# Whole 128-row tiles, GpSimd drains and adding transfers in a pooled-attention and mixture-of-experts kernel

## The chip, the cores and the metric

The kernel runs on one core of a Trainium2 chip. The metric is the device time of one execution in microseconds (us). Engines are TensorE (matrix products), VectorE, ScalarE, GpSimd (POOL in the rows) and SyncE (SP), which here only issues transfers. Data moves by 16 DMA engines, fed by a hardware queue (transfers issued on SyncE) and a software queue (transfers issued on GpSimd).

## The reference

Attention with pooled keys and values over 8 batches of 8 heads, 576 tokens and a head width of 64, then a mixture of 8 experts with top-1 routing, then a three-way gated layer, all in float32:

```python
k_p = k.reshape(B, H, Sp, pool, D).mean(axis=3)      # pool = 8, Sp = 72
v_p = v.reshape(B, H, Sp, pool, D).mean(axis=3)
scores = scale * np.matmul(q, k_p.transpose(0, 1, 3, 2))
attn = np.exp(scores - np.max(scores, axis=-1, keepdims=True))
attn = attn / (np.sum(attn, axis=-1, keepdims=True) + 1e-09)
x = np.matmul(attn, v_p)                             # then [4608, 512]
# experts: xn @ en.T / tau, argmax, gate = softmax at the argmax
out[mask] = gate_w[mask, None] * (np.maximum(x[mask] @ w1[e], 0.0) @ w2[e])
# second layer
h = np.maximum(np.maximum(x @ w1, x @ w2), x @ w3);  result = h @ w_out
```

## The kernel before

Three stages follow each other. **Attention** takes 36 tiles of 128 query rows. The 576 pooled key rows of a batch (8 heads by 72) lie in five chunks of 128, 128, 128, 128 and 64 rows (`RC`). One turn of `for it in range(NT + 4)` issues stages of several tiles: scores (`stage_s`, names `psc`), exponentials (`stage_e`), transposes of the weights into `paT` and the copy into `aT` (`stage_a`), transposes of the queries (`stage_q`, `pqT`), and the product of `aT` with the values (`stage_x`, `pav`, L496). VectorE takes the row maxima, subtracts them and scales the result (L457 to L523), and beside that works on the routing of earlier tiles. A float32 pass of TensorE appears twice in the rows, a transpose once.

The values stand in `vbds`, spread out over head slots with a column of ones and 8 columns for the routing logits (73 columns a head). Chunk 4 has 64 rows and one head, so two of a tile's twelve recorded `pav` passes, and parts of `trans_kv` (L318), `trans_v` (L341) and `vdot` (L350), use 64 of the array's 128 rows.

**Pooling** is a sum over 8 rows. `load_rows` brings a batch's keys (`kraw`) and values (`vraw`) on SyncE, 1,024 KB and 128 KB each. For the first batches VectorE reduces part of it; from there GpSimd adds halves of each row three times (`pool_k2`, `pool_v`: w = 4, 2, 1, that is 256, 128 and 64 columns), chunk by chunk. Then `spread_v` (L293) writes the values to `vbds`. `kraw` and `vraw` have two buffers each, so a load waits for the adds of the batch two before it. The dictionary `todo` holds for each `it` the jobs of a batch; a batch b is first needed on TensorE at `need = (b // 2) * 9 + (0 or 4)`. On GpSimd everything runs in the order in which it was issued.

**The experts** (L1062, L1110) follow, and then **the second layer** (`second`) in 6 groups of 768 tokens: nine chunks of products, then six output tiles j = 0 to 5 of a group (`out_part`, L1697), each scaled by ScalarE (L1703) and written by an indirect scatter that GpSimd issues (`out_rows`, L1704). After the last group the kernel ends with drains and semaphores of all engines (rows with L1802).

Of the kernel before, what the change touches and what calls it, by code (L numbers as in the profile page):

```python
# [21 lines left out]
def attention_moe_moe_kernel(  # L22
# [32 lines left out]
    J = 8  # L55
# [60 lines left out]
    if True:  # L116
# [61 lines left out]
        if True:  # L178
# [7 lines left out]
            kv = {}  # L186

            def load_rows(pool_tag, src, b, sizes, apart=False, step=4):
                t = kvp.tile([P, 5, J, D], F32, tag=pool_tag, name=f"{pool_tag}{b}")
                flat = src[b].rearrange("h (s j) d -> (h s) (j d)", j=J)  # L190
                full = 0 if apart else sum(1 for n in sizes if n == P)
                for c in range(0, full, step):
                    e_ = min(c + step, full)
                    nc.sync.dma_start(
                        t[:, c:e_].rearrange("p c j d -> p c (j d)"),
                        flat[c * P : e_ * P].rearrange("(c p) x -> p c x", p=P),
                    )
# [37 lines left out]
            kbds = [ap1.tile([P, H, 2, SP], F32, name=f"kbd{i}") for i in range(3)]  # L235
            vbds = [ap1.tile([P, NSL, DA], F32, name=f"vbd{i}") for i in range(3)]
            nc.gpsimd.memset(kbds[0], 0.0)
            rmask = ap1.tile([P, 5, H], F32, name="rmask")
# [15 lines left out]
            def prep_steps(b):  # L254
                kt, vt = kv[b]
                kb, vb = kbds[b % 3], vbds[b % 3]
                kp = qp.tile([P, 5, 2, D], F32, tag="kp", name=f"kp{b}")
                vp = kp[:, :, 1, :] if b > 1 else qp.tile([P, 5, D], F32, tag="vp", name=f"vp{b}")
                vT = qp.tile([D, 5, P], F32, tag="vT", name=f"vT{b}", bufs=1)

# [12 lines left out]
                def pool_k2(sizes=RC, c0=0):  # L273
                    for c, n in list(enumerate(sizes))[c0:]:
                        for w in (4, 2, 1):
                            dst = kt[0:n, c, 0:w, :] if w > 1 else kp[0:n, c, 0:1, :]
                            nc.gpsimd.tensor_tensor(dst, kt[0:n, c, 0:w, :], kt[0:n, c, w : 2 * w, :], op=A.add)
# [5 lines left out]
                def pool_v(c0, c1, n):  # L283
                    for c in range(c0, c1):
                        for w in (4, 2, 1):
                            dst = vt[0:n, c, 0:w, :] if w > 1 else vp[0:n, c : c + 1, :]
                            nc.gpsimd.tensor_tensor(dst, vt[0:n, c, 0:w, :], vt[0:n, c, w : 2 * w, :], op=A.add)
# [24 lines left out]
                def trans_kv(cs, r0):  # L312
# [3 lines left out]
                    for c in cs:  # L316
                        n = RC[c]
                        nc.tensor.transpose(  # L318
                            ps[:, col : col + n], kp[0:n, c].rearrange("p two d -> p (two d)"), ident[0:n, 0:n]
                        )  # L320
                        col += n
                    a0 = 0
                    while a0 < col:
# [10 lines left out]
                        a0 = a1  # L334
                    nc.scalar.copy(vT.rearrange("p c r -> p (c r)")[:, r0 : r0 + col], ps[D:P, 0:col])

                def trans_v(c0, c1):
                    ps = pq.tile([P, 512], F32, tag="pq", name=f"ptv{b}_{c0}")
                    for c in range(c0, c1):
                        n = RC[c]  # L340
                        nc.tensor.transpose(  # L341
                            ps[0:D, (c - c0) * P : (c - c0) * P + n], vp[0:n, c, :], ident[0:n, 0:n]
                        )
                    w_ = (c1 - c0 - 1) * P + RC[c1 - 1]
                    nc.scalar.copy(vT.rearrange("p c r -> p (c r)")[:, c0 * P : c0 * P + w_], ps[0:D, 0:w_])

                def vdot():
                    ps = pq.tile([P, 512], F32, tag="pq", name=f"pd{b}")
                    for c, (h0, h1) in enumerate(HS):
                        nc.tensor.matmul(  # L350
                            ps[0 : RC[c], SL[c] * E : SL[c + 1] * E],
                            vT[:, c, 0 : RC[c]],
                            enT[:, h0:h1, :].rearrange("p h e -> p (h e)"),
                            start=True,
                            stop=True,
                        )
                    for n, s0, s1 in ((P, 0, SL[4]), (64, SL[4], NSL)):
                        nc.vector.tensor_tensor(
                            vb[0:n, s0:s1, D + 1 : DA],
                            ps[0:n, s0 * E : s1 * E].rearrange("p (s e) -> p s e", e=E),  # L360
                            mslot[0:n, s0:s1, :].to_broadcast([n, s1 - s0, E]),
                            op=A.mult,
                        )

# [103 lines left out]
            def stage_a(i):  # L468
# [3 lines left out]
                for c, n in enumerate(RC):  # L472
                    nc.tensor.transpose(ps[0:n, c * P : (c + 1) * P], at[:, c * P : c * P + n], ident)
                aT = ap2.tile([P, 5, P], F32, tag="aT", name=f"aT{i}")
                nc.scalar.copy(aT[:, 0:4, :], ps[:, 0 : 4 * P].rearrange("p (c n) -> p c n", n=P))
# [12 lines left out]
            def stage_x(i):  # L488
# [892 lines left out]
            p0[0]()  # L1381
            enT = ap1.tile([D, H, E], F32, name="enT")

            def en_steps():
# [4 lines left out]
                for h in range(H):  # L1389
                    nc.tensor.transpose(ps[0:D, h * E : (h + 1) * E], en[:, h * D : (h + 1) * D], ident[0:E, 0:E])  # L1390
                nc.scalar.copy(enT, ps[0:D, 0 : H * E].rearrange("p (h e) -> p h e", e=E))

# [75 lines left out]
            for b in range(1, B):  # L1468
                need = (b // 2) * 9 + (0 if b % 2 == 0 else 4)
                at_ = [need - 7, need - 3, need - 1, need, need, need + 1, need + 2]  # L1470
                at_ = {1: [2, 4, 6, 7], 2: [5, 6, 6, 7, 7, 7, 8, 9, 10]}.get(b, at_[:4] + at_[5:6])
                for j, t in enumerate(at_):
                    todo.setdefault(t, []).append((b, j))
# [7 lines left out]
            for it in range(NT + 4):  # L1481
# [90 lines left out]
    def second(st, groups, again=False):  # L1572
# [144 lines left out]
        for g in groups:  # L1717
# [89 lines left out]
```

## Time and profile before

| | us |
|---|---|
| median of 3 runs (1242.42 to 1244.53) | 1244.08 |
| profiled execution | 1242.23 |
| its span | 1240.2 |
| granted clock, mean (share of 2.4 GHz) | 0.995 |

| engine | busy us | share of the span |
|---|---|---|
| TensorE | 1205.1 | 97% |
| VectorE | 795.3 | 64% |
| ScalarE | 579.9 | 47% |
| GpSimd | 318.1 | 26% |

The span runs from the first instruction to the last; the profiled execution's own time is 2.0 us longer. Busy shares are means over stages. TensorE's weight loads (PEld) overlap its matrix passes, and the ends of passes are modelled, so that gaps are read better from the starts of weight loads. "[0.27 <-issue]" behind a row is idle time before it and what ended it; "issue" means that nothing in the profile released it. A shape like 64\*128 is the rows by columns of the array that are used.

### The profile page before, as it was taken

The page shows a single profiled execution, that of the slowest core. Times are in us where ns is not written, and L with a number is a line of the kernel's source. Part 1 is how long each engine was busy: PE and PEld are TensorE (multiplying, and loading weights), DVE is VectorE, ACT ScalarE, POOL GpSimd, SP SyncE. Part 2 cuts the span into 40 slices and gives each one's busy share as a digit, 9 for nine tenths or more (in the row PEclk, how much of TensorE's full clock was granted, in tenths as well). Part 3 has the DMA queues.
Part 4 walks back from the last instruction along what each step waited for, and adds up shares of the span by engine and source line. Part 5 has one row for each costly group of instructions (what it writes and reads, how often), then busy time and mean ns, then how long its engine had stood idle before and what let it go on. Part 6 is the DMA issues. An engine that isn't in the chain of part 4 may idle for free. (4 is left out here: it accounts for less than half of the span.)

```text
span 1240.2 us, 22423 instructions
## 1 busy us (share of the span) xinstructions
PE 1205.1 (97%) x8251; PEld 1149.6 (93%) x8251; DVE 795.3 (64%) x1597; ACT 579.9 (47%) x1040; POOL 318.1 (26%) x471
## 2 busy tenths in 40 slices
PE   6999999999999999999999999999999999999995
PEld 5888889899999999999998998998998998998994
DVE  5878886977789999987854445454454454453540
ACT  4666574445566666666654323324223223233221
POOL 6999534401122212121001202003004004004001
PEclk9999999999999999999999999999999999999998
DMA  9796344607884456555349665574673773773721
GB/s 261 222 341 205 137 145 155 198 23 138 296 279 154 138 213 221 205 204 158 124 146 307 253 241 209 193 254 173 231 264 146 256 262 122 259 286 107 262 97 53
DMA packets 98054, 246.21 MB, mean 199 GB/s; under 512 B 17116, under 2 KB 58122, under 8 KB 89874
## 3 DMA queue, kind: packets, MB, share of 16 engines
q1 hardware_dynamic: 84786, 189.09, 45.0%
q0 software_dynamic: 13152, 55.62, 13.4%
q8 instruction: 67, 1.10, 0.4%
q14 instruction: 49, 0.40, 0.1%
HBM read 252.23 MB, written 46.98 MB: 241 GB/s over the span
## 5 line engine op out<-in xcount | busy, mean ns | idle before, releaser
L1621 PE MATMUL p<-yhi,wt 128*128 128x384 f32 x1512 | 387.1, 336 | 0.0
L1621 PEld LDWEIGHTS p<-yhi,wt 128*128 128x128 f32 x1512 | 273.4, 188 | 0.7 <-PE pyT L1132 0.3
L1621 PE MATMUL p<-ylo,wt 128*128 128x384 f32 x756 | 254.0, 336 | 0.0
L1629 ACT COPY s<-p 128x384 f32<-128x384 f32 x162 | 77.8, 480 | 221.6 <-PE p L1621 214.2
L1110 PE MATMUL py<-hhi,wlo 128*128 128x256 f32 x576 | 163.1, 283 | 1.6 <-DVE wlo L1042 1.6
L1110 PE MATMUL py<-hhi,whi 128*128 128x256 f32 x576 | 164.6, 286 | 0.0
L1062 PE MATMUL ph<-xhi,whi 128*128 128x256 f32 x576 | 163.8, 284 | 0.7 <-DVE hlo L1078 0.7
L1062 PE MATMUL ph<-xhi,wlo 128*128 128x256 f32 x576 | 163.0, 283 | 0.7 <-DVE wlo L1042 0.7
L1062 PE MATMUL ph<-xlo,whi 128*128 128x256 f32 x576 | 163.0, 283 | 0.0
L1110 PE MATMUL py<-hlo,whi 128*128 128x256 f32 x576 | 162.9, 283 | 0.0
L1621 PEld LDWEIGHTS p<-ylo,wt 128*128 128x128 f32 x756 | 142.1, 188 | 0.5
L1650 DVE TENSOR_TENSOR blk<-p,s 128x384 f32<-128x384 f32 x108 | 59.7, 553 | 113.8 <-PE p L1621 113.5
L1606 POOL DMA_INDIRECT gt<-gbuf,ix x26 | 37.0, 1423 | 315.6 <-DMA ix<-idbuf 309.2
L1110 PEld LDWEIGHTS py<-hhi,wlo 128*128 128x128 f32 x576 | 110.4, 192 | 1.8 <-DVE wlo L1042 1.8
L1062 PEld LDWEIGHTS ph<-xhi,whi 128*128 128x128 f32 x576 | 110.5, 192 | 1.3 <-DVE hlo L1078 1.1
L1062 PEld LDWEIGHTS ph<-xhi,wlo 128*128 128x128 f32 x576 | 110.5, 192 | 0.9 <-DVE wlo L1042 0.9
L1062 PEld LDWEIGHTS ph<-xlo,whi 128*128 128x128 f32 x576 | 110.5, 192 | 0.0
L1110 PEld LDWEIGHTS py<-hlo,whi 128*128 128x128 f32 x576 | 110.5, 192 | 0.0
L1110 PEld LDWEIGHTS py<-hhi,whi 128*128 128x128 f32 x576 | 110.4, 192 | 0.0
L1042 DVE TENSOR_TENSOR wlo<-w2raw,whi 128x1024 fp32r<-128x1024 f32 x84 | 102.1, 1220 | 8.6 <-ACT whi L1040 8.5
L1042 DVE TENSOR_TENSOR wlo<-w1raw,whi 128x1024 fp32r<-128x1024 f32 x67 | 81.7, 1219 | 26.2 <-ACT whi L1040 25.3
L1040 ACT CAST whi<-w2raw 128x1024 fp32r<-128x1024 f32 x88 | 91.8, 1043 | 7.4 <-PE py L1110 4.4
(317 smaller groups left out, 2260.1 us busy)
## 6 DMA issues: line engine op xcount, KB each, us to landing
wt<-wdram SPq DMA_DIRECT2D x51, 1792.0 KB
w1raw<-in_moe_w_dram SPq DMA_DIRECT2D x88, 512.0 KB
w2raw<-in_moe_w_dram SPq DMA_DIRECT2D x88, 512.0 KB
wdram<-wst POOLq DMA_DIRECT2D x9, 1792.0 KB
ybuf<-yo SPq DMA_DIRECT2D x40, 256.0 KB
cvraw<-in_moe_w_dram POOLq DMA_DIRECT2D x36, 256.0 KB
xbuf<-x SPq DMA_DIRECT2D x16, 512.0 KB
yr<-ybuf SPq DMA_DIRECT2D x20, 384.0 KB
```

Of the source, the lines that this page charges most:

```text
L1040: nc.scalar.copy(hi, src)
L1042: eng.tensor_tensor(lo, src, hi.bitcast(F32), op=A.subtract)
L1062: nc.tensor.matmul(ps[:, f, :], a_[:, c, fs], b_[:, c, :], start=(n == 0), stop=(n == 3 * DC - 1))
L1110: nc.tensor.matmul(py[:, c // 2, (c % 2) * 256 : (c % 2 + 1) * 256], a_[:, f, c * P : (c + 1) * P], b_[:, f, :], start=(piece == 0 and f = ...
L1606: nc.gpsimd.indirect_dma_start(out=gt[g][:, j : j + 1], out_offset=None, in_=gbuf[:, :], in_offset=bass.IndirectOffsetOnAxis(ap=cols[j], a ...
L1621: nc.tensor.matmul(ps, a_, b_, start=(start and c + n == 0), stop=(c == 1 and n == 2), skip_group_check=True)
L1629: nc.scalar.copy(t, ps)
L1650: tt(src, add[0], add[1], op=A.add)
```

## The change

Three things change. First, what had 64 rows now has 128: `aT`, `kp`, `vp`, `vT`, `enT` and the last slots of `vbds` are fixed buffers whose unused rows are set to zero at the start, and the passes on them (`trans_kv`, `trans_v`, `vdot`, `pav`) run over all 128 rows. `vT` and `enT` keep their data in rows 64 to 127. The two VectorE products behind `vdot` become one.

Second, GpSimd gets a `drain` after the fourth output tile of each of the six groups.

Third, from the fourth batch on (b of 3 to 7) SyncE loads only the first 4 of the 8 rows to be summed, as pieces of 1 KB, and GpSimd issues four transfers a batch that add the other 4 rows to them in the buffer (`accum_op`), 20 in all. GpSimd then adds only twice (w = 2, 1). The transfers are issued in the turn `need - 9`.

```diff
+            HJ = J // 2
+            NFULL = 3
+            def row_parts(src, b, t, j0):
+                flat = src[b].rearrange("h (s j) d -> (h s) j d", j=J)
+                yield (
+                    t[:, 0:4, 0:HJ].rearrange("p c j d -> p c (j d)"),
+                    flat[0 : 4 * P, j0 : j0 + HJ].rearrange("(c p) j d -> p c (j d)", p=P),
+                )
+                yield t[0 : RC[4], 4, 0:HJ].rearrange("p j d -> p (j d)"), flat[4 * P :, j0 : j0 + HJ].rearrange("p j d -> p (j d)")
+            def load_half(pool_tag, src, b):
+                t = kvp.tile([P, 5, J, D], F32, tag=pool_tag, name=f"{pool_tag}{b}")
+                for dst, rows_ in row_parts(src, b, t, 0):
+                    nc.sync.dma_start(dst, rows_)
+                return t
+            def add_half(src, b, t):
+                for dst, rows_ in row_parts(src, b, t, HJ):
+                    nc.gpsimd.dma_start(dst, rows_, accum_op=A.add)
...
+            aTs = [ap1.tile([P, 5, P], F32, name=f"aT{i}") for i in range(2)]
+            kps = [qp.tile([P, 5, 2, D], F32, name=f"kp{i}", bufs=1) for i in range(2)]
...
+            for t_ in aTs:
+                nc.vector.memset(t_[R4:P, 4, :], 0.0)
+            for t_ in vbds:
+                nc.vector.memset(t_[R4:P, SL[4] : NSL, :], 0.0)
...
-                        for w in (4, 2, 1):
+                        for w in (4, 2, 1) if b < NFULL else (2, 1):
...
-                            ps[:, col : col + n], kp[0:n, c].rearrange("p two d -> p (two d)"), ident[0:n, 0:n]
+                            ps[:, col : col + P], kp[:, c].rearrange("p two d -> p (two d)"), ident
...
-                            ps[0 : RC[c], SL[c] * E : SL[c + 1] * E],
-                            vT[:, c, 0 : RC[c]],
+                            ps[:, SL[c] * E : SL[c + 1] * E],
+                            vT[:, c, :],
...
-                    for n, s0, s1 in ((P, 0, SL[4]), (64, SL[4], NSL)):
-                        nc.vector.tensor_tensor(
...
+                    nc.vector.tensor_tensor(
+                        vb[:, :, D + 1 : DA],
...
-                                aT[0 : RC[c], c, lo:hi],
-                                vbds[b % 3][0 : RC[c], sl : sl + g1 - g0, :].rearrange("p h d -> p (h d)"),
+                                aT[:, c, lo:hi],
+                                vbds[b % 3][:, sl : sl + g1 - g0, :].rearrange("p h d -> p (h d)"),
...
+                if b >= NFULL:
+                    todo.setdefault(need - 9, []).append(
+                        lambda b=b: (add_half(k, b, kv[b][0]), add_half(v, b, kv[b][1]))
+                    )
...
-                    kv[kvnext] = (load_rows("kraw", k, kvnext, RC), load_rows("vraw", v, kvnext, RC))
+                    if kvnext < NFULL:
+                        kv[kvnext] = (load_rows("kraw", k, kvnext, RC), load_rows("vraw", v, kvnext, RC))
+                    else:
+                        kv[kvnext] = (load_half("kraw", k, kvnext), load_half("vraw", v, kvnext))
...
                 out_rows(g, p_, j)
+                if j == 3:
+                    nc.gpsimd.drain()
```

The order of TensorE's 7,742 passes, and of SyncE's transfers, stays the same. On GpSimd two places matter. The first is behind the spread of batch 1 (`vbd_168`), where before the adds of batch 2's values (`vraw_257`) came at once:

```order
L293 TENSOR_TENSOR vbd_168<-vp_350,mslot 128x2x64
L293 TENSOR_TENSOR vbd_168<-vp_350,mslot 128x3x64 x3
L293 TENSOR_TENSOR vbd_168<-vp_350,mslot 64x64
L287 TENSOR_TENSOR vraw_257<-vraw_257 128x256
L287 TENSOR_TENSOR vraw_257<-vraw_257 128x128
L287 TENSOR_TENSOR kp_530<-vraw_257 128x64
```

In the changed kernel the adding transfers of batch 3 (`kraw_391`, `vraw_394`) stand between; batch 2's values are called `vraw_273` there:

```order
L330 TENSOR_TENSOR vbd_168<-vp_175,mslot 128x2x64
L330 TENSOR_TENSOR vbd_168<-vp_175,mslot 128x3x64 x3
L330 TENSOR_TENSOR vbd_168<-vp_175,mslot 64x64
L207 DMA kraw_391<-in_k_dram 128x4x256
L207 DMA kraw_391<-in_k_dram 64x256
L207 DMA vraw_394<-in_v_dram 128x4x256
L207 DMA vraw_394<-in_v_dram 64x256
L324 TENSOR_TENSOR vraw_273<-vraw_273 128x256
L324 TENSOR_TENSOR vraw_273<-vraw_273 128x128
L324 TENSOR_TENSOR kp_172<-vraw_273 128x64
```

So four issues, and their waits for SyncE's loads of batch 3, stand ahead of batch 2's adds. The second place is between batches 3 and 4 on GpSimd; before, the spreads of batch 2 (`vbd_169`) and batch 3 (`vbd_167`) were followed by batch 4's keys (`kraw_646`):

```order
L293 TENSOR_TENSOR vbd_169<-kp_530,mslot 128x2x64
L293 TENSOR_TENSOR vbd_169<-kp_530,mslot 128x3x64 x3
L293 TENSOR_TENSOR vbd_169<-kp_530,mslot 64x64
L293 TENSOR_TENSOR vbd_167<-kp_614,mslot 128x2x64
L293 TENSOR_TENSOR vbd_167<-kp_614,mslot 128x3x64 x3
L293 TENSOR_TENSOR vbd_167<-kp_614,mslot 64x64
L277 TENSOR_TENSOR kraw_646<-kraw_646 128x256
L277 TENSOR_TENSOR kraw_646<-kraw_646 128x128
L277 TENSOR_TENSOR kp_936<-kraw_646 128x64
```

Now the transfers of batch 4 (`kraw_644`, `vraw_647`) are issued between the two spreads, and batch 4's adds follow:

```order
L330 TENSOR_TENSOR vbd_169<-kp_172,mslot 128x2x64
L330 TENSOR_TENSOR vbd_169<-kp_172,mslot 128x3x64 x3
L330 TENSOR_TENSOR vbd_169<-kp_172,mslot 64x64
L207 DMA kraw_644<-in_k_dram 128x4x256
L207 DMA kraw_644<-in_k_dram 64x256
L207 DMA vraw_647<-in_v_dram 128x4x256
L207 DMA vraw_647<-in_v_dram 64x256
L330 TENSOR_TENSOR vbd_167<-kp_173,mslot 128x2x64
L330 TENSOR_TENSOR vbd_167<-kp_173,mslot 128x3x64 x3
L330 TENSOR_TENSOR vbd_167<-kp_173,mslot 64x64
L314 TENSOR_TENSOR kraw_644<-kraw_644 128x128
L314 TENSOR_TENSOR kp_172<-kraw_644 128x64
```

Only one spread lies between the issue of a batch's adding transfers and its first add, and the 256-column add is gone. Batches 5 to 7 repeat this.

## Rows read from the trace of the kernel before

**Rows 1.** The page, busy time of each engine over the span

```profile
PE 1205.1 (97%) x8251; PEld 1149.6 (93%) x8251; DVE 795.3 (64%) x1597; ACT 579.9 (47%) x1040; POOL 318.1 (26%) x471
```

**Rows 2.** Busy time by stretch: us, engines, granted clock, DMA share, GB/s

```profile
62.00:93.00 31.00, 30.80 (x249) 27.78 (x248) 23.49 (x65) 19.25 (x49) 28.64 (x62) 1.00 1.06 341
186.00:217.00 31.00, 31.00 (x251) 30.24 (x252) 18.66 (x36) 15.27 (x25) 13.43 (x9) 1.00 0.46 155
```

**Rows 3.** Timeline of TensorE's weight loads, one tile: start, duration, group

```profile
104.88 0.47 PEld L417 LDWEIGHTS pqT<-ident,qgrp 128*128 128x128 f32 x4
105.31 1.40 PEld L496 LDWEIGHTS pav<-vbd,aT 128*128 128x128 f32 x10
106.98 0.29 PEld L496 LDWEIGHTS pav<-vbd,aT 64*128 64x128 f32 x2 [0.27 <-issue]
107.35 1.03 PEld L442 LDWEIGHTS psc<-kbd,qT 128*128 128x128 f32 x8
...
108.87 0.47 PEld L417 LDWEIGHTS pqT<-ident,qgrp 128*128 128x128 f32 x4
```

**Rows 4.** Weight loads grouped by shape, 0 to 190 us: busy, mean | idle

```profile
L496 PEld LDWEIGHTS pav<-vbd,aT 64*128 64x128 f32 x60 | 8.8, 184 | 8.1 <-issue 8.1
```

**Rows 5.** Busy time by stretch, three attention tiles

```profile
37.63:42.49 4.86, 4.68 (x37) 4.05 (x35) 4.86 (x13) 2.77 (x8) 4.57 (x10) 1.00 1.04 317
104.88:108.87 3.99, 3.99 (x31) 3.65 (x29) 2.58 (x7) 2.42 (x6) 3.54 (x8) 1.00 0.97 267
157.91:163.00 5.09, 4.65 (x41) 3.81 (x39) 4.99 (x24) 3.87 (x12) 3.77 (x5) 1.00 0.25 103
```

**Rows 6.** Timeline of VectorE, the start

```profile
4.01 1.94 DVE L263 TENSOR_REDUCE kp<-kraw 128x64 f32<-128x512 f32 x2 [2.90 <-DMA kraw<-in_k_dram]
```

**Rows 7.** Line L1802: ns min/median/max, first and last start

```profile
L1802 POOLq DRAIN  x3: 46/109/6689, 1232.7 to 1239.9; - x3
```

**Rows 8.** Timeline of GpSimd, the end

```profile
1220.59 0.98 POOL L1704 DMA_INDIRECT out_dram<-ob,ix  x1 [2.52 <-DMA out_dram<-ob,ix]
1224.09 0.98 POOL L1704 DMA_INDIRECT out_dram<-ob,ix  x1 [2.52 <-ACT ob L1703]
1228.08 0.98 POOL L1704 DMA_INDIRECT out_dram<-ob,ix  x1 [3.01 <-ACTq L1761]
```

**Rows 9.** GpSimd's adds grouped by shape, 0 to 190 us

```profile
L287 POOL TENSOR_TENSOR vraw<-vraw 128x256 f32<-128x256 f32 x30 | 21.9, 729 | 6.6 <-DMA vraw<-in_v_dram 6.6
...
L287 POOL TENSOR_TENSOR vraw<-vraw 128x128 f32<-128x128 f32 x30 | 13.7, 458 | 2.4
...
L287 POOL TENSOR_TENSOR kp<-vraw 128x64 f32<-128x64 f32 x24 | 7.8, 323 | 1.9
```

**Rows 10.** Timeline of GpSimd, batches 1 to 3 and the last stores

```profile
37.48 2.04 POOL L293 TENSOR_TENSOR vbd<-vp,mslot 128x128 f32<-128x128 f32 x5
...
47.38 0.32 POOL L287 TENSOR_TENSOR kp<-vraw 64x64 f32<-64x64 f32 x1
...
63.55 0.31 POOL L287 TENSOR_TENSOR kp<-vraw 64x64 f32<-64x64 f32 x1
...
138.61 3.14 POOL L1488 DMA_DIRECT2D ybuf<-ones  x4
```

**Rows 11.** Timeline of SyncE's issues: start, duration, line, transfer

```profile
37.54 0.37 SPq L194 DMA_DIRECT2D vraw<-in_v_dram  x1
...
55.81 0.37 SPq L194 DMA_DIRECT2D kraw<-in_k_dram  x1
```

**Rows 12.** DMA, 62 to 93 us: total; hardware queue (packets, MB, share)

```profile
DMA packets 6787, 10.58 MB, mean 341 GB/s; under 512 B 1325, under 2 KB 3373, under 8 KB 6783
...
q1 hardware_dynamic: 6783, 10.53, 105.5%
```

**Rows 13.** Timeline of weight loads: transposes for batches 2 and 7

```profile
52.35 0.42 PEld L318 LDWEIGHTS ptk<-ident,kp 128*128 128x128 f32 x4
...
155.99 0.42 PEld L318 LDWEIGHTS ptk<-ident,kp 128*128 128x128 f32 x4
```

More of the change, by code (lines that the diff above doesn't have):

```diff
@@ L236, in attention_moe_moe_kernel @@
             vbds = [ap1.tile([P, NSL, DA], F32, name=f"vbd{i}") for i in range(3)]
+            R4 = RC[4]
+            aTs = [ap1.tile([P, 5, P], F32, name=f"aT{i}") for i in range(2)]
+            kps = [qp.tile([P, 5, 2, D], F32, name=f"kp{i}", bufs=1) for i in range(2)]
+            vps = [qp.tile([P, 5, D], F32, name=f"vp{i}", bufs=1) for i in range(2)]
+            vT = qp.tile([P, 5, P], F32, name="vT", bufs=1)
+            enT = ap1.tile([P, H, E], F32, name="enT")
+            for t_ in kps:
+                nc.vector.memset(t_[R4:P, 4], 0.0)
+            for t_ in vps:
+                nc.vector.memset(t_[R4:P, 4, :], 0.0)
+            nc.vector.memset(vT[0:D], 0.0)
+            nc.vector.memset(vT[D:P, 4, R4:P], 0.0)
+            nc.vector.memset(enT[0:D], 0.0)
+            for t_ in aTs:
+                nc.vector.memset(t_[R4:P, 4, :], 0.0)
+            for t_ in vbds:
+                nc.vector.memset(t_[R4:P, SL[4] : NSL, :], 0.0)
             nc.gpsimd.memset(kbds[0], 0.0)
@@ L256, in prep_steps @@
                 kb, vb = kbds[b % 3], vbds[b % 3]
-                kp = qp.tile([P, 5, 2, D], F32, tag="kp", name=f"kp{b}")
-                vp = kp[:, :, 1, :] if b > 1 else qp.tile([P, 5, D], F32, tag="vp", name=f"vp{b}")
-                vT = qp.tile([D, 5, P], F32, tag="vT", name=f"vT{b}", bufs=1)
+                kp = kps[b % 2]
+                vp = kp[:, :, 1, :] if b > 1 else vps[b]
                 def pool_k(c):
@@ L284, in pool_v @@
                     for c in range(c0, c1):
-                        for w in (4, 2, 1):
+                        for w in (4, 2, 1) if b < NFULL else (2, 1):
                             dst = vt[0:n, c, 0:w, :] if w > 1 else vp[0:n, c : c + 1, :]
@@ L316, in trans_kv @@
                     for c in cs:
-                        n = RC[c]
                         nc.tensor.transpose(
-                            ps[:, col : col + n], kp[0:n, c].rearrange("p two d -> p (two d)"), ident[0:n, 0:n]
+                            ps[:, col : col + P], kp[:, c].rearrange("p two d -> p (two d)"), ident
                         )
-                        col += n
+                        col += RC[c]
                     a0 = 0
@@ L334, in trans_kv @@
                         a0 = a1
-                    nc.scalar.copy(vT.rearrange("p c r -> p (c r)")[:, r0 : r0 + col], ps[D:P, 0:col])
+                    nc.scalar.copy(vT[D:P].rearrange("p c r -> p (c r)")[:, r0 : r0 + col], ps[D:P, 0:col])
                 def trans_v(c0, c1):
@@ L339, in trans_v @@
                     for c in range(c0, c1):
[L340 to L343, printed above, removed]
+                        nc.tensor.transpose(ps[0:D, (c - c0) * P : (c - c0 + 1) * P], vp[:, c, :], ident)
                     w_ = (c1 - c0 - 1) * P + RC[c1 - 1]
-                    nc.scalar.copy(vT.rearrange("p c r -> p (c r)")[:, c0 * P : c0 * P + w_], ps[0:D, 0:w_])
+                    nc.scalar.copy(vT[D:P].rearrange("p c r -> p (c r)")[:, c0 * P : c0 * P + w_], ps[0:D, 0:w_])
                 def vdot():
@@ L356, in vdot @@
                         )
-                    for n, s0, s1 in ((P, 0, SL[4]), (64, SL[4], NSL)):
-                        nc.vector.tensor_tensor(
[L359 to L363, printed above, removed]
+                    nc.vector.tensor_tensor(
+                        vb[:, :, D + 1 : DA],
+                        ps[:, 0 : NSL * E].rearrange("p (s e) -> p s e", e=E),
+                        mslot.to_broadcast([P, NSL, E]),
+                        op=A.mult,
+                    )
                 if b == 0:
@@ L473, in stage_a @@
                     nc.tensor.transpose(ps[0:n, c * P : (c + 1) * P], at[:, c * P : c * P + n], ident)
-                aT = ap2.tile([P, 5, P], F32, tag="aT", name=f"aT{i}")
+                aT = aTs[i % 2]
                 nc.scalar.copy(aT[:, 0:4, :], ps[:, 0 : 4 * P].rearrange("p (c n) -> p c n", n=P))
@@ L1381, in attention_moe_moe_kernel @@
             p0[0]()
-            enT = ap1.tile([D, H, E], F32, name="enT")
             def en_steps():
@@ L1390, in en_steps @@
                     nc.tensor.transpose(ps[0:D, h * E : (h + 1) * E], en[:, h * D : (h + 1) * D], ident[0:E, 0:E])
-                nc.scalar.copy(enT, ps[0:D, 0 : H * E].rearrange("p (h e) -> p h e", e=E))
+                nc.scalar.copy(enT[D:P], ps[0:D, 0 : H * E].rearrange("p (h e) -> p h e", e=E))
             tok_i = rp.tile([P, NT], I32, name="tok_i")
@@ L1471, in attention_moe_moe_kernel @@
                 at_ = {1: [2, 4, 6, 7], 2: [5, 6, 6, 7, 7, 7, 8, 9, 10]}.get(b, at_[:4] + at_[5:6])
+                if b >= NFULL:
+                    todo.setdefault(need - 9, []).append(
+                        lambda b=b: (add_half(k, b, kv[b][0]), add_half(v, b, kv[b][1]))
+                    )
                 for j, t in enumerate(at_):
```

## The prediction, made before the changed kernel was run

> **What bounds the kernel now.** I read the page's busy times first: TensorE works for 97% of the span, GpSimd for 26% [rows 1]. Such shares are means over stages, so the busy time by stretch came next. TensorE is busy for 30.80 of the 31 us between 62 and 93 us, where VectorE has 23.49, GpSimd 28.64 and the DMA engines are full, and for all 31 us once the experts run [rows 2]. So TensorE sets the time nearly everywhere, and the change touches TensorE's passes only in attention. But "busy" holds pauses too, since the ends of passes are modelled. The timeline of weight loads shows them by their starts: a plain tile runs from 104.88 to 108.87, 3.99 us, and inside it the two 64-row passes of `pav` are preceded by 0.27 us in which nothing else released them [rows 3]. Third, GpSimd's timeline and the transposes that need its sums show how much room pooling has. Last, the end: after the last scatter at 1228.08 [rows 8] no engine computes, yet the span runs to 1240.2, and a GpSimd drain of 6.689 us begins at or after 1232.7 [rows 7].
>
> **Whole tiles.** The number of passes stays, and no pass streams more columns; what can go is the pause at the change between 128 and 64 rows. In the tile of [rows 3] the ten whole passes of `pav` start at 105.31 and take 1.40, 0.14 each; the next product starts at 107.35. The two 64-row passes thus own 107.35 - 105.31 - 1.40 = 0.64 us, where two whole passes at 0.14 would take 0.28: a gain of 0.36 a tile. The lower bound is the 0.27 of idle time alone; over all of attention the 64-row form has 8.1 us of it in front of 60 passes, that is 30 tiles [rows 4].
>
> Not every tile can use it. The same tile has VectorE busy for 2.58 of 3.99 us, but others have none to spare: 4.86 of 4.86 between 37.63 and 42.49, 4.99 of 5.09 from 157.91 [rows 5]. Going through the tiles one by one, I count ten of 36 with under 0.3 us of VectorE idle, those two being the first and the last. There VectorE sets the pace and the gain is put at nothing. The sum is 26 x 0.36 = 9.4 us; the bounds are 26 x 0.27 = 7.0 and 36 x 0.36 = 13.0. Of what is added, the memsets lie at the start, where VectorE waits 2.90 us for the first keys [rows 6]; without that cover they would cost a few tenths each. The two products behind `vdot` becoming one saves VectorE one short operation a batch, counted at nothing.
>
> **Drains.** No semaphore wait goes with them. The three GpSimd drains of the end took 6,689, 109 and 46 ns [rows 7]; the two short ones had no transfer issued on GpSimd since the drain ahead of them, the long one nearly all of the run's. I read this as work left over from such transfers which the drain pays for, so that a drain in each group pays most of it earlier, where GpSimd waits anyway. Two scatters remain behind the last new drain, so I leave 0.5 us, between the 0.11 of a drain with nothing before it and the old price: a gain of 6.2. In the last group the new drain stands between the scatters of 1220.59 and 1224.09; GpSimd is idle for 2.52 us there [rows 8], and a drain of a few tenths hides in it. The bounds are 6.6 gained (6.69 - 0.11) and, if every drain costs 6.69 whatever was issued, a loss: the last drain stays, and the fifth scatter waits until 1220.59 + 0.98 + 6.69 = 1228.26 instead of 1224.09, so the end comes 4.2 later.
>
> **Adding transfers.** GpSimd loses ten adds a batch of 0.73 us, 7.3 us, and keeps 0.46 + 0.32 per chunk [rows 9]. Before, batch 3's adds ran from 47.38 + 0.32 to 63.55 + 0.31, 16.2 us [rows 10]; now 8.9. It gains four issues, priced by the four 256 KB stores of 3.14 us [rows 10], also issued on GpSimd. No wait of TensorE on GpSimd stands on its path, so less work there gains nothing directly; what counts is whether the sums come late.
>
> Batch 3's four issues stand in front of batch 2's value adds, and behind the issues' waits are queued those adds and all that follows. SyncE issues batch 3's values at 37.54 [rows 11] and GpSimd ends batch 1's spread at 39.52 [rows 10], so the wait for the half load is about a microsecond, and batch 2's adds end some 3.5 to 4.5 us later than 47.70, at 51.2 to 52.2. The transposes start at 52.35 [rows 13], or about 2 us earlier once tiles are faster; they want the fifth chunk (1.6 us of adds) later. That leaves 0 to 1.5 us of waiting; I take 1.0.
>
> From there a batch costs GpSimd 3.1 (issues) + L + 8.9, where L is the time from the last issue until the transfers have landed; the spread of 2.04 us [rows 10] runs beside L. Batch 3 ends at 51.2 + 8.9 = 60.1, batch 2's spread at 62.1 and batch 4's issues at 65.3; batch 4 ends at 74 + L, batch 5 at 86 + 2L, 6 at 98 + 3L, 7 at 110 + 4L. Batch 7 is needed at 155.99 [rows 13], now about 148, so no L under 9.5 us costs anything, and each us above costs up to 4. No transfer that adds is in the trace. The nearest rows are copies: the hardware queue fills the engines at 341 GB/s [rows 12], at which half of a batch's keys and values (1.18 MB) takes 3.5 us, and a scatter's landing kept GpSimd idle for 2.52 [rows 8]. That makes L about 6, the lower bound and the value that I take; the upper bound is a quarter of the rate, L = 16.3. What SyncE no longer loads, GpSimd's transfers load through the same 16 engines, so copying gains nothing.
>
> The engines stay full between 62 and 93 us [rows 12], and nothing in the trace says that adding is free. The Trainium skill speaks against it: "Collectives: The Full Stack", section "The bandwidth ceiling: the fold count and why AG ≠ RS ≠ AR", says that an add inside a transfer needs two source reads, and that reduce-scatter therefore runs at half of all-gather's rate. By that rule the 3.5 us would be 6.9 and L 9.4, just at the point where it begins to cost; the sum would stay and the rival below would gain weight. No run here shows it.
>
> **The sum.** 1242.23 - 9.4 - 6.2 + 1.0 + 0 = 1227.6 for an execution like the profiled one. The median of the runs is 1.85 above the profiled execution, which makes 1229.5; I say 1229.
>
> **Rivals.**
> - *The drain at the end stays as it is.* For it: it comes after the last landing, and one long drain can't show what it depends on. Against it: 109 and 46 ns for the other two. Time: 1229.5 + 6.2 = 1235.7, and up to 1240 if each drain costs as much.
> - *VectorE takes TensorE's place as the bound in attention.* For it: the full tiles of [rows 5]; faster tiles bring the next VectorE step forward. Against it: 1.41 us idle in the plain tile. The gain falls from 9.4 to some 5: 1234. The change not doing what it says belongs here: if the 0.27 us isn't due to the 64 rows, the gain is nothing and the time 1239.
> - *The transfers land late but not very late*, L between 9.5 and 13: 1231 to 1244.
> - *Slower: the adding transfers bind GpSimd.* The mechanism is GpSimd's order: the issue of a batch's transfers, one spread, then adds that need the landing, and the next batch's issues behind these. With a quarter of the copy rate L = 16.3, and 4 x (16.3 - 9.5) = 27 us: 1256. The gains elsewhere are 14.6 us, so it decides from L = 9.5 + 14.6 / 4 = 13. For it: full engines in [rows 12], a wait in the order of GpSimd that wasn't there, four of them in a row. Against it: GpSimd's own work falls by 4 us a batch, and the engines are at half share from 186 on, but that is too late for it.
>
> **Chances.** The forecast 0.46 (its own range 1224 to 1233), the drain unchanged 0.17, the smaller gain of whole tiles 0.08, late landing 0.09 (half of it faster), bound by transfers 0.20. Faster by over 0.2% (2.5 us, about what a measurement of this kernel can tell from no change) is 0.46 + 0.17 + 0.08 + 0.05 = 0.76, no change 0.04 from the late landings, slower 0.20. The range reaches from 1222 (the upper bounds of both gains, 13.0 and 6.6, and no wait, 1224.5, less the scatter of runs) to 1250, which is L = 14.6 and leaves about half of the slower rival out.
>
> **What would show it.** Whole tiles: a plain tile of 3.63 us and no idle before `pav`'s last two passes; wrong if the idle stays or VectorE shows none in plain tiles. Drains: six in the second layer, each under a few us, and a last one under 1 us; wrong if the last is still 6.7. Adding transfers: GpSimd's wait before a batch's first add under 7 us, and no transpose of pooled rows waiting for GpSimd; wrong if waits of 10 us or more stand there. The experts and the second layer up to the last group should keep their durations; a change there would mean that I have missed something.

## The result and the profile after

The changed kernel takes 1225.5 us (median of 4 runs, 1225.17 to 1226.15) against 1244.3; the ratio is 0.9845, 95% interval 0.982 to 0.987. Forecast were 1229 and a range of 1222 to 1250. The profiled execution's span is 1223.3 us against 1240.2. Cut at the first transpose of queries, at the first product of the experts and at TensorE's last pass, the 16.9 us lie here:

| us | before | after | difference |
|---|---|---|---|
| to the first query transpose | 12.01 | 11.13 | -0.9 |
| attention | 174.23 | 164.90 | -9.3 |
| experts and second layer, to TensorE's end | 1040.80 | 1041.23 | +0.4 |
| from there to the span's end | 13.18 | 6.07 | -7.1 |

Attention and the end hold the gain, as forecast. The page after, first the busy times and then the software queue (packets, MB, share), answers to [rows 1]:

```profile
PE 1194.4 (98%) x8251; PEld 1149.6 (94%) x8251; DVE 791.5 (65%) x1601; ACT 578.9 (47%) x1040; POOL 308.9 (25%) x441
...
q0 software_dynamic: 19232, 61.52, 16.8%
```

GpSimd does 30 operations fewer (50 adds less, 20 issues more) and is busy for 308.9 us instead of 318.1. The stretches of [rows 2], in the same columns:

```profile
62.00:93.00 31.00, 30.33 (x262) 29.52 (x261) 24.07 (x73) 21.91 (x56) 22.20 (x44) 1.00 1.00 256
186.00:217.00 31.00, 30.31 (x252) 30.09 (x251) 23.20 (x44) 15.75 (x23) 14.20 (x7) 1.00 0.46 153
```

GpSimd fell from 28.64 to 22.20 us between 62 and 93 us, and the DMA engines stay full, at 256 GB/s instead of 341. In these 31 us a packet of 1 KB that adds took 104 ns on average, a copied one of the same size 53 ns (before: 53 ns). The tile that answers to [rows 3]:

```profile
100.63 0.47 PEld L449 LDWEIGHTS pqT<-ident,qgrp 128*128 128x128 f32 x4
101.06 1.77 PEld L528 LDWEIGHTS pav<-vbd,aT 128*128 128x128 f32 x12
102.75 1.04 PEld L474 LDWEIGHTS psc<-kbd,qT 128*128 128x128 f32 x8
...
104.28 0.47 PEld L449 LDWEIGHTS pqT<-ident,qgrp 128*128 128x128 f32 x4
```

The twelve passes of `pav` are one group, with no idle ahead of the last two, and the tile takes 104.28 - 100.63 = 3.65 us. The end answers to [rows 7] and [rows 8]: the six new drains (line L1781), those at the very end (L1841; duration min/median/max in ns), and the last three scatters.

```profile
L1781 POOLq DRAIN  x6: 3241/3636/8476, 761.9 to 1210.6; - x6
```

```profile
L1841 POOLq DRAIN  x3: 46/109/208, 1221.8 to 1223.0; - x3
```

```profile
1210.87 0.99 POOL L1741 DMA_INDIRECT out_dram<-ob,ix  x1 [2.56 <-DMA out_dram<-ob,ix]
1214.74 0.99 POOL L1741 DMA_INDIRECT out_dram<-ob,ix  x1 [2.89 <-ACT ob L1740]
1218.43 0.98 POOL L1741 DMA_INDIRECT out_dram<-ob,ix  x1 [2.70 <-ACTq L1800]
```

The longest drain at the end is 0.208 us, not 6.689. The new drains take 3.2 to 8.5 us each, which includes the scatter issued into them; in the last group the fifth scatter starts 3.87 us after the fourth, where it was 3.50 before.

GpSimd in the middle of attention, where [rows 10] stood before: the four issues of batch 5, a spread, and the first adds of keys and of values.

```profile
83.39 2.20 POOL L207 DMA_DIRECT2D kraw<-in_k_dram  x2
84.73 3.09 POOL L207 DMA_DIRECT2D vraw<-in_v_dram  x2
86.09 3.78 POOL L330 TENSOR_TENSOR vbd<-kp,mslot 128x128 f32<-128x128 f32 x5
91.91 0.45 POOL L314 TENSOR_TENSOR kraw<-kraw 128x128 f32<-128x128 f32 x1 [2.05 <-PE paT L505]
...
97.17 0.45 POOL L324 TENSOR_TENSOR vraw<-vraw 128x128 f32<-128x128 f32 x1 [0.86 <-DMA vraw<-in_v_dram]
```

GpSimd is ready at 89.87 and waits 2.05 us before the keys' adds; for the values it waits 0.86. (The first wait is put down to TensorE, whose pass had long ended; the keys' landing is the likelier releaser.) The issues take 2.7 us of GpSimd and then slow the spread, from 2.04 to 3.78 us. The longest wait of TensorE for GpSimd in attention is at batch 2's transposes (two more, of 0.39 and 0.42 us, are put down to GpSimd):

```profile
49.57 0.31 PEld L354 LDWEIGHTS ptk<-ident,kp 128*128 128x128 f32 x3
51.27 0.14 PEld L354 LDWEIGHTS ptk<-ident,kp 128*128 128x128 f32 x1 [1.39 <-POOL kp L324]
```

It is 1.39 us long; forecast was 1.0. What it costs is taken up at `e7_from_batch4`.

### The profile page after: what moved, and what is told of

Read it like the earlier page. It is cut to its first block, busy times and chain, and to the rows that moved or that the text cites. A ratio compares the mean times of both kernels' runs of the same rounds, so it can differ in the third digit from the quotient of the medians.

```text
span 1223.3 us, 22433 instructions
## 1 busy us (share of the span) xinstructions
PE 1194.4 (98%) x8251; PEld 1149.6 (94%) x8251; DVE 791.5 (65%) x1601; ACT 578.9 (47%) x1040; POOL 308.9 (25%) x441
## 5 line engine op out<-in xcount | busy, mean ns | idle before, releaser
L1074 DVE TENSOR_TENSOR wlo<-w2raw,whi 128x1024 fp32r<-128x1024 f32 x84 | 102.3, 1222 | 9.2 <-ACT whi L1072 9.2
```

What stands on the lines that cost most here:

```text
L1074: eng.tensor_tensor(lo, src, hi.bitcast(F32), op=A.subtract)
```

## The experiments

Twelve more runs were made, in three series of four, each beside the kernel before (median 1243.6, 1242.62 and 1244.06). `c1_changed` is the changed kernel once more; `e5_light_adds` and `e6_copying`, which leave out half of each sum, are not in the table but told below. W are the whole tiles, D the drains, T the adding transfers. Attention and end are those of the profiled execution, cut as above; "last drain" is the longest at the very end.

| run | parts | median us | ratio to before, interval | attention | end | last drain |
|---|---|---|---|---|---|---|
| before | none | 1244.3 | | 174.23 | 13.18 | 6.69 |
| w_tiles_alone | W | 1234.49 | 0.9919 (0.990 to 0.9937) | 167.41 | 13.18 | 6.69 |
| d_drains_alone | D | 1234.85 | 0.9924 (0.9907 to 0.9942) | 175.11 | 5.66 | 0.21 |
| t_transfers_alone | T | 1235.28 | 0.9934 (0.9915 to 0.9953) | 170.23 | 9.23 | 3.18 |
| e1_full_loads | W D | 1227.93 | 0.9867 (0.9847 to 0.9888) | 167.75 | 6.12 | 0.21 |
| e2_no_drains | W T | 1229.1 | 0.9877 (0.9856 to 0.9898) | 166.47 | 9.14 | 3.18 |
| e3_half_tiles | D T | 1231.68 | 0.9905 (0.9886 to 0.9924) | 172.33 | 6.06 | 0.21 |
| changed | W D T | 1225.5 | 0.9845 (0.982 to 0.987) | 164.90 | 6.07 | 0.21 |
| c1_changed | W D T | 1226.28 | 0.9866 (0.9843 to 0.9889) | 164.95 | 6.09 | 0.21 |
| e7_from_batch4 | W D, T from batch 4 | 1226.2 | 0.9858 (0.9833 to 0.9882) | 165.69 | 5.79 | 0.21 |
| e4_one_drain | W T, first drain only | 1229.9 | 0.9887 (0.9869 to 0.9905) | 167.38 | 10.95 | 4.62 |
| l_drain_last_group | W T, last group's drain only | 1228.33 | 0.9871 (0.9849 to 0.9893) | 165.49 | 8.49 | 0.21 |

The last drain comes out the same to 0.01 us wherever the same transfers precede it. Attention doesn't: W with T has 164.90 to 167.38 in five executions whose attention is the same program. A difference of 2 us between two single profiles of attention is not shown by them.

Most of that scatter lies in the first nine tiles, though. Cut once more at the tenth group of query transposes, attention divides so (us, one figure for each profiled execution):

| parts | first nine tiles | from the tenth tile on |
|---|---|---|
| none (before, `d_drains_alone`) | 42.29, 43.31 | 131.94, 131.80 |
| W (`w_tiles_alone`, `e1_full_loads`) | 42.62, 42.71 | 124.79, 125.04 |
| T (`t_transfers_alone`, `e3_half_tiles`) | 40.24, 42.94 | 129.99, 129.39 |
| W T (the five executions) | 41.10 to 44.04 | 123.13 to 123.85 |

From the tenth tile on the four groups don't overlap. By their means whole tiles bring 7.0 us there without the transfers and 6.1 beside them, the transfers 2.2 us without whole tiles and 1.3 beside them. In the first nine tiles no gain of either can be told from the scatter.

TensorE's clock differs there too. In five executions of the upper table (before, `w_tiles_alone`, `e1_full_loads`, `e7_from_batch4`, `e4_one_drain`) the granted clock falls to the lower of its two levels, 1.2 GHz, for 3.4 us between 46 and 56 us, shortly after TensorE paused for 0.7 to 1.5 us; in `d_drains_alone` it doesn't fall, after pauses of 0.72 and 1.32 us. No cost of it shows: the eighth and ninth tile take 11.81 us in before, with the fall, and 11.82 in `d_drains_alone`, the same program in attention, and VectorE is busy for all of the 10.40 us from 40.0 to 50.4 in both.

**Leaving one part out.** `e1_full_loads` (no T):

```diff
-            NFULL = 3
+            NFULL = 8
```

> The changed kernel with whole loads for all batches: no adding transfers, GpSimd adds three times again; whole tiles and drains stay. Theory (the adding transfers shorten nothing that TensorE waits for, and cost the 1.4 us that TensorE waits for batch 2's sums): 1224.1 us, no wait of a transpose for GpSimd, plain tiles still 3.65 us. Rival (the faster tiles need a faster GpSimd, which only the adding transfers give): a wait for GpSimd at batches 4 to 7 and 1228 to 1231 us.

Measured 1227.93, and no wait of TensorE for pooled sums of batches 2 to 7. So the rival's wait isn't there, but neither is the gain that the theory expected: attention is 167.75, longer than in each of the five executions with transfers, by 0.4 to 2.9 us.

`e2_no_drains`:

```diff
                 out_rows(g, p_, j)
-                if j == 3:
-                    nc.gpsimd.drain()
```

> The changed kernel without the six drains. Theory (the drain at the end pays for all transfers that GpSimd issued since the last one): the last drain takes 6.7 us again and the semaphore step ahead of it 1.8, 1232.5 us in all. Rival (the end got shorter for another reason, such as the earlier end of attention): the last drain stays below 1 us and the time at 1225.5.

Measured 1229.1. The drain at the end comes back, but at 3.18 us, the semaphore step at 0.96: neither 6.7 nor under 1.

```profile
L1839 POOLq DRAIN  x3: 46/109/3177, 1223.9 to 1227.6; - x3
```

`e3_half_tiles` (the kernel before with D and T; without the padding and its memsets, and with the old operands):

```diff
-                                aT[:, c, lo:hi],
-                                vbds[b % 3][:, sl : sl + g1 - g0, :].rearrange("p h d -> p (h d)"),
+                                aT[0 : RC[c], c, lo:hi],
+                                vbds[b % 3][0 : RC[c], sl : sl + g1 - g0, :].rearrange("p h d -> p (h d)"),
```

> The kernel before with the drains and the adding transfers, but with 64-row operands as before. Theory (the pause around the 64-row passes is worth 9 us in attention): plain tiles of 4.00 us with 0.27 us idle before the last two passes of pav, 1234 us. Rival (VectorE sets the pace of attention and the gain comes from the transfers' lighter load): plain tiles near 3.7 us and 1228 us.

Measured 1231.68. A plain tile, by its weight loads:

```profile
104.92 0.47 PEld L438 LDWEIGHTS pqT<-ident,qgrp 128*128 128x128 f32 x4
...
107.02 0.29 PEld L517 LDWEIGHTS pav<-vbd,aT 64*128 64x128 f32 x2 [0.27 <-issue]
...
108.92 0.47 PEld L438 LDWEIGHTS pqT<-ident,qgrp 128*128 128x128 f32 x4
```

The pause is back and the tile takes 4.00 us, so the pause belongs to the 64 rows. But the time is 2.3 us below the 1234 that 9 us for whole tiles would make of it.

**The drain's price.** `e4_one_drain`:

```diff
-                if j == 3:
+                if j == 3 and g == 0:
```

> The changed kernel with one drain only, in the first of the six groups. Theory (a price per transfer issued since the drain before): 57 of 177 transfers are left for the end, so the last drain takes about 2.2 us, the semaphore step ahead of it 0.6, and the time is 1227.5 us. Rival (a drain is short only when another one stands shortly ahead of it): 6.7 us at the end and 1232 us.

Measured 1229.9; the end's drain:

```profile
L1841 POOLq DRAIN  x3: 46/109/4622, 1224.8 to 1230.0; - x3
```

After 57 transfers (counted by their starts in the trace; in the kernel's order they are 56, as the fourth scatter starts inside the drain) it is 4.62 us, where the 197 of `e2_no_drains` gave 3.18 and the 177 of the kernel before 6.689. The price per transfer since the last drain is refuted as I had put it, and so is the rival, which had it back at 6.7. The drain in the first group doesn't go by the number of transfers alone either: 8.48 us with 140 of them ahead of it, 20 of these adding, 6.84 with the same 140 where the 20 copy (`e6_copying`), and 4.03 with whole loads (120). `d_drains_alone`, an edit of the kernel before:

```diff
                 out_rows(g, p_, j)
+                if j == 3:
+                    nc.gpsimd.drain()
```

> The kernel before with the six drains only. Theory: the first drain 4.0 us as with whole loads (120 transfers ahead of it), the others 3.2 to 3.9, the last one 0.21; attention as before; 7 us below the kernel before. Rival (drains in the middle delay the second layer by what the end saves): no change.

```profile
L1744 POOLq DRAIN  x6: 3227/3622/4029, 772.3 to 1220.9; - x6
```

Measured 1234.85, the first drain 4.029 us, the last 0.21, as expected. The gain is in the end alone: 13.18 to 5.66 us, with attention at 175.11. `l_drain_last_group`:

```diff
-                if j == 3:
+                if j == 3 and g == groups[-1]:
```

> The changed kernel with one drain only, in the last of the six groups. Theory (a drain's price depends on how far the software queue has come, as the 3.2 us of the run without drains): that drain takes 3.0 for the work left plus the 2.8 us that a drain there needs at least, about 6 us, delays the fifth scatter by some 2.5, and the time is 1 to 2 us above the changed kernel, 1227 to 1228. Rival (73 ns for each transfer since the last drain, 194 of them): 2.8 + 14 = 17 us, and 1236.

```profile
L1781 POOLq DRAIN  x1: 4229/4229/4229, 1211.4 to 1211.4; - x1
```

Measured 1228.33; the drain takes 4.23 us, and the price per transfer (17 us) is out once more. My 6 was too high: scatter, landing and what is left over seem to run beside each other in it. A price that rises by about 0.08 us per transfer (57 of them: 4.62 - 0.11) and falls back each time the queue has taken a certain amount would fit the drains at the end. That is a guess: no run counted what the queue had taken, and the 6.84 us after copies show that the number of transfers is not the whole measure.

**What the transfers bring.** `e5_light_adds` (whole loads; GpSimd leaves out its 256-column adds from batch 3 on, and with them half of each sum):

```diff
-            NFULL = 3
+            NFULL = 8
...
-                        for w in (4, 2, 1) if b < NFULL else (2, 1):
+                        for w in (4, 2, 1) if b < 3 else (2, 1):
```

> The changed kernel with whole loads and no adding transfers, but GpSimd still skips its 256-column adds from batch 3 on; the second half of each of those sums is left out of the result. New theory (fewer GpSimd adds stretch VectorE's routing operations less, and that is what the adding transfers bring): the routing operation on 72 columns keeps a mean near 0.25 us, the wait for batch 2 is gone, and the time is 1 to 2 us below the changed kernel in this series. Rival (the lighter hardware queue or the order of the transfers brings it): 2 us above the changed kernel, as with whole loads and all adds.

The whole time, 1391.56 us, says nothing: with other sums the tokens go to other experts, and a branch for more expert items runs. Attention isn't touched by that and takes 165.31 us, with the mean of the 72-column routing operation at 258 ns as in the changed kernel, against 167.75 and 371 with all adds. Over the whole of attention these 2.4 us are within the scatter noted above. From the tenth tile on it takes 123.61 us, inside the range of the executions with adding transfers (123.13 to 123.85) and outside that of whole loads with all adds (124.79 and 125.04). So there the fewer adds bring the gain without the lighter hardware queue, as the theory had it.

The parts by themselves say it more clearly. `w_tiles_alone`, as an edit of the changed kernel:

```diff
-            NFULL = 3
+            NFULL = 8
...
-                if j == 3:
-                    nc.gpsimd.drain()
```

> The kernel before with whole tiles only. Theory (64-row passes cost 0.35 us a tile, in tiles that TensorE paces): attention 167.8 us from the first query transpose to the first expert product instead of 174.2, the last drain 6.7 us as before, since the same 177 transfers are issued on GpSimd; 6.5 us below the kernel before. Rival (whole tiles give all of 9.4 us, and the other parts nothing in attention): attention 165 us, 9.4 below.

Measured 1234.49: attention 167.41 and a last drain of 6.69, as the theory had it. The time is 9.6 us below, though (interval 8 to 12), where 6.5 was expected. The profiled execution is 8.3 us shorter: 6.8 in attention and 1.2 ahead of the first query transpose, where the executions scatter from 10.8 to 12.0. `t_transfers_alone` (the kernel before with `load_half`, `add_half` and the shorter adds):

```diff
-                        for w in (4, 2, 1):
+                        for w in (4, 2, 1) if b < NFULL else (2, 1):
...
+                    kv[kvnext] = (load_half("kraw", k, kvnext), load_half("vraw", v, kvnext))
```

> The kernel before with the adding transfers only. Theory (fewer GpSimd adds free VectorE's routing operations; the last drain depends on how far the software queue has come, not on the number of transfers): attention 172.3 us instead of 174.2, the last drain 3.2 us as in the run without drains, 6 us below the kernel before. Rival (the transfers bring nothing; the drain pays per transfer and 197 are more than 177): attention 174, last drain 7.4 us, no change.

Measured 1235.28, 8.8 below. The profiled execution is 7.2 us shorter: 4.0 from the end (the drain at 3.18, as in `e2_no_drains`) and 4.0 from attention, less 1.0 in the experts and the second layer. Two of attention's 4.0 lie from the tenth tile on, and 1.5 of these have a place. In the kernel before, VectorE in one tile:

```profile
119.58 0.22 DVE L553 TENSOR_TENSOR pre<-pre 128x72 f32<-128x72 f32 x1
...
120.44 2.85 DVE L553 TENSOR_TENSOR pre<-pre 128x72 f32<-128x72 f32 x1
123.21 0.15 DVE L506 TENSOR_SCALAR rs<-pav 128x8 f32<-128x8 f32 x1
```

and GpSimd at that time:

```profile
120.47 2.04 POOL L293 TENSOR_TENSOR vbd<-kp,mslot 128x128 f32<-128x128 f32 x5
122.47 1.25 POOL L277 TENSOR_TENSOR kraw<-kraw 128x256 f32<-128x256 f32 x2
```

The routing operation on 72 columns, 0.22 us long a moment earlier, takes 2.85 us while GpSimd runs a spread without a pause. VectorE's next step of the tile starts only at 123.21; the tile after it, from 122.92 to 129.13, takes 6.20 us, and 4.67 with the transfers alone. The two groups of VectorE over attention, before and with the transfers alone:

```profile
L460 DVE TENSOR_TENSOR sh<-psc,mx 128x576 f32<-128x576 f32 x34 | 25.7, 756 | 2.1
...
L553 DVE TENSOR_TENSOR pre<-pre 128x72 f32<-128x72 f32 x8 | 5.2, 653 | 0.0
```

```profile
L481 DVE TENSOR_TENSOR sh<-psc,mx 128x576 f32<-128x576 f32 x35 | 26.5, 757 | 2.4 <-DVE ohs L683 0.2
...
L574 DVE TENSOR_TENSOR pre<-pre 128x72 f32<-128x72 f32 x8 | 2.4, 304 | 0.0
```

The subtraction that reads its scores from PSUM keeps its 756 ns; the one with both operands in SBUF falls from 653 to 304. So fewer GpSimd operations, and at other times, give VectorE time back. Whole tiles move the two apart as well (368 ns in `w_tiles_alone`), so this part of the gain belongs to either change and counts once. The Trainium skill has the rule: "GPSIMD Engine Reference", section "1. Specifications", says that GpSimd shares its SBUF interfaces with VectorE, with contention where a VectorE instruction has two SBUF inputs. These rows agree. In `d_drains_alone`, the same program in attention, the operation takes 2.84 us again, and in both executions it starts within 0.03 us of the spread. No run moved the spread alone, so that the spread holds VectorE up is argued from this and from the rule.

`e7_from_batch4`:

```diff
-            NFULL = 3
+            NFULL = 4
```

> The changed kernel with the adding transfers from batch 4 on, not 3. Theory (batch 3's four issues ahead of batch 2's adds cost the 1.4 us that TensorE waits for them): no such wait, and 1 to 1.4 us below the changed kernel. Rival (batch 3's whole adds stretch VectorE's operations by as much): the same time.

Measured 1226.2 beside 1226.28 for the changed kernel in that series, where it ran unedited as `c1_changed`:

> The changed kernel once more, as the reference for the other three of this series: 1225.5 us, and the same last drain of 0.21 us.

The wait for batch 2 is gone and the time is the same, as the rival had it. But the rival's reason, that batch 3's whole adds cost as much, isn't shown. Rather, the wait seems to have cost nothing: VectorE has no pause there. The stretch in the changed kernel, then in this run:

```profile
40.00:50.40 10.40, 9.48 (x83) 8.53 (x82) 10.39 (x34) 5.45 (x14) 9.76 (x15) 1.00 1.01 242
```

```profile
40.00:50.40 10.40, 9.33 (x64) 8.83 (x66) 10.40 (x38) 5.74 (x14) 9.42 (x20) 0.84 0.72 231
```

VectorE (the third busy time) is busy for 10.39 and 10.40 of 10.40 us. The eighth and ninth tile, where the wait stood, take 11.71 us without it (with the fall of the clock, 0.84 on average here) and 11.61 in the changed kernel with it.

`e6_copying` (half of each sum is left out):

```diff
-                    nc.gpsimd.dma_start(dst, rows_, accum_op=A.add)
+                    nc.gpsimd.dma_start(dst, rows_)
```

> The changed kernel with the same 20 transfers on GpSimd, but copying over the first half instead of adding to it, so that half of each sum is left out of the result. By two source reads for an add, GpSimd's waits for batches 4 to 6 (4.3 + 1.6, 2.1 + 0.9, 3.5 + 1.2 us) shrink by 3 to 4 us each, and the time stays within 1 us, since no wait of TensorE hangs on them. Rival (an add costs a transfer no more than a copy, the waits come from full engines): the same waits.

Measured 1228.35 (interval 0.9861 to 0.9907), with attention at 162.89; as other sums change the routing, only attention is compared. The software queue between 38 and 134 us, first adding, then copying (packets, MB, share of 16 engines over 96 us):

```profile
q0 software_dynamic: 6080, 5.90, 39.3%
```

```profile
q0 software_dynamic: 2080, 6.95, 23.6%
```

Adding takes 0.393 x 96 / 5.90 = 6.4 us of all engines per MB, copying 0.236 x 96 / 6.95 = 3.3: a factor of 2.0. The upper bound of the prediction was four. (The copying row holds the four stores of 256 KB too.) But the copies went as packets of 4 KB and the adds as packets of 1 KB, so the size could be the cause. Single packets speak against that: in the same 96 us of the changed kernel the hardware queue's copied packets of 1 KB took 55 ns on average and the adding ones 104, a factor of 1.9. Nor is it the queue, as copied packets of 4 KB have the same median, 159 ns, on both (`e6_copying`). The Trainium skill's rule of two source reads ("Collectives: The Full Stack", section "The bandwidth ceiling: the fold count and why AG ≠ RS ≠ AR") agrees with these numbers; that the second read is the reason is not shown here. The waits shrank less than expected: for the keys of batches 4 to 6 they are 3.21, 0 and 1.43 us, against 3.27, 2.13 and 2.33 in `c1_changed`; engines that other loads fill are part of both. The issues became cheaper too, and the spread behind them isn't slowed; whether that is due to copying or to a quarter of the packets isn't told apart:

```profile
75.05 1.33 POOL L207 DMA_DIRECT2D kraw<-in_k_dram  x2
76.37 1.32 POOL L207 DMA_DIRECT2D vraw<-in_v_dram  x2
77.70 2.04 POOL L330 TENSOR_TENSOR vbd<-kp,mslot 128x128 f32<-128x128 f32 x5
```

## Why the prediction was right, and where it was not

The time and the sign came out, since two errors of the sum cancelled: by the means of attention whole tiles brought 5.4 us beside the transfers, 4.0 less than forecast, and the transfers alone took 3.4 us off where 1.0 was to be added. That these errors are nearly equal is luck.

- **Whole tiles, -9.4 forecast, 5 to 7 measured.** The size per tile was right (0.36 forecast; 4.00 to 3.65 us), and `e3_half_tiles` shows that the pause goes with the 64 rows. The step that failed is "26 x 0.36". Alone, whole tiles take 6.8 us off attention (174.23 to 167.41), and 1.9 of them are the tile behind the stretched VectorE operation (6.20 to 4.32; beside the transfers 4.67 to 4.32); beside the transfers the means are 171.3 (two runs) and 165.8 (five), 5.4 less. Comparing tile by tile, before against `w_tiles_alone`, 17 got shorter by 0.28 to 0.35, not 26, and three got longer by 0.30 to 0.35. VectorE's idle time did not pick them: of the ten tiles that I had set to nothing, three (from 76.81, 117.83 and 153.52) gained that much as well, and of the other 26 only 14 did. I had taken VectorE for the only other limit. In the three that got longer, which mix two batches (the fourth such tile changed by 0.06), it is ScalarE's copy of the queries. First before, then `e1_full_loads`:

```profile
72.23 0.47 PEld L417 LDWEIGHTS pqT<-ident,qmix 128*128 128x128 f32 x4
...
75.03 1.09 PEld L428 LDWEIGHTS psc<-kbd,qT 128*64 128x64 f32 x16 [0.34 <-ACT qT L418]
...
76.81 0.47 PEld L417 LDWEIGHTS pqT<-ident,qgrp 128*128 128x128 f32 x4
```

```profile
71.23 0.47 PEld L449 LDWEIGHTS pqT<-ident,qmix 128*128 128x128 f32 x4
...
74.37 1.09 PEld L460 LDWEIGHTS psc<-kbd,qT 128*64 128x64 f32 x16 [0.87 <-ACT qT L450]
...
76.16 0.47 PEld L449 LDWEIGHTS pqT<-ident,qgrp 128*128 128x128 f32 x4
```

The wait for `qT` grows from 0.34 to 0.87 us, and the turn from 4.58 to 4.93: it got longer.
- **Drains, -6.2 forecast, -7.1 measured** (13.18 to 6.07), and -7.5 alone. Right in place and size, helped by the semaphore step ahead of the drain (1.81 to 0.24 us), which I had not counted. The mechanism, a price per transfer issued, was wrong: fewer transfers gave 4.62 and more gave 3.18. I took the remainder from a rule that one long drain can't bear out, as the rival said. The rival's own case, a drain at the end that stays, did not come.
- **Adding transfers, +1.0 forecast.** The stall at batch 2 is there (1.39 us), but no cost of it shows in `e7_from_batch4`. The step that failed is that less work on GpSimd "gains nothing directly": alone the transfers took 4.0 us off attention (3.4 by the means of two executions each), 1.5 of them in the tile after the 2.85 us operation. Beside whole tiles what is left is 165.8 (five runs) against 167.6 (two), 1.7 us, about the scatter; from the tenth tile on it is 1.3, more than the scatter there. The row of 2.85 us was in the trace before; I had read VectorE's busy time in [rows 5] as work.
- **The slower rival** did not come. It needed L of 13 us. Batches 4 to 6 ended at 83.4, 101.2 and 120.5, that is 17.8 and 19.3 us apart; less the 12.0 us of GpSimd's own work in the forecast that leaves 5.8 and 7.3 for L, against 6 forecast and 9.5 to begin to cost. Batch 7 did not wait.
- **The smaller gain of whole tiles** was the rival nearest to the truth in its mechanism, another engine in TensorE's place, but the other terms made up for it.

## What to carry to other kernels

Before pricing an engine's busy time as work, look for operations of one form that last several times their usual time, and at what the neighbour engine does then; less work there can be worth more than its share of the path. When a stretch is bound by one engine, count for each tile which engine comes next, all of them, before multiplying a gain per tile by the tiles. And measure parts alone as well as left out: here the parts alone gain 9.6, 9.2 and 8.8 us, and all three together 18.8 (16.3 in the second series), not 27.6. In the profiled executions the end shows it best: the drains alone shorten it by 7.5 us, the transfers alone by 4.0, all three together by 7.1.

## What the runs showed that was not expected

- The price of a GpSimd drain at the end depends on the transfers issued there before in a way that isn't monotonic: 3 of them (2 in the kernel's order) 0.21 us, 57 4.62, 177 6.69, 197 3.18; equal programs repeat it to 0.01 us. What it goes by, and why it falls back, stays open.
- Behind the issue of adding transfers GpSimd stays slow: the spread behind takes 3.78 us, and 2.04 behind the same transfers as copies, in a quarter of the packets.
- An adding transfer takes 2.0 times the engine time per byte of a copy, 1.9 times for packets of the same 1 KB.
